# Parameters made in two parts by channel, the first for the first two chunks of the generation

## The chip, the cores and the metric

One core of one Trainium2 chip. The core has TensorE (PE), VectorE (DVE), ScalarE (ACT), GpSimd (POOL) and SyncE (SP), which issues DMAs; GpSimd and ScalarE issue DMAs too. Each engine works through its own instructions in order and waits on semaphores for the others. The metric is the device time of one execution in microseconds; shorter is better.

## The reference

Two branches over one sequence of 2,048 tokens and 640 channels are mixed by a gate. Branch A is attention of 32 heads over a window of 8 positions, two apart. Branch B is a state space layer: a long kernel K per channel, made from 192 complex states, then convolved with the input by FFT.

```python
def _A_ref(x, wqkv, wo):
    qkv = (x @ wqkv)                       # q, k, v: H = 32, Dh = 20
    logits = einsum("bhsd,bhswd->bhsw", q, kg) * Dh ** -0.5   # W = 8, dil = 2
    attn = softmax(where(mask, logits, -1e9))
    return einsum("bhsw,bhswd->bhsd", attn, vg) @ wo

def _B_ref(u, A_re, A_im, B_re, B_im, C_re, C_im, log_dt, Dskip):
    dt = exp(log_dt)
    P = exp(dt * (A_re + 1j * A_im) * l)   # 640 x 192 states x 2048
    K = einsum("dn,dnl,dn->dl", C, P, dt * B).real
    y = irfft(rfft(u padded) * rfft(K padded))[:L] + u * Dskip
...
g = sigmoid((x * gate_w).sum(-1, keepdims=True))
return g * _A_ref(x, ...) + (1 - g) * _B_ref(x, ...)
```

## The kernel before

The program has three stretches. In the first, `SSMParams.build` turns the six parameter arrays into 12 bfloat16 "pieces" per state: phase, phase times 256, log decay, log size and angle, each split into two or three parts (`split`, `piece`). It works on all 640 channels at once, as tiles of 128 partitions by 5 x 192 columns (the 960-wide instructions). Each piece is copied on ScalarE (L352) and written to the DRAM buffer `Sprm` by SP (L353). Between its 22 steps stand the steps of `Attn.window`: transposes of x on TensorE (L86) with copies to `xT` on ScalarE (L87), the projections to q, k and v of the first 1,024 tokens (L117, copies of two at a time at L119, written to DRAM by GpSimd at L122), and the gate (L93 to L105).

In the second stretch, `KGen.chunk` generates the long kernel in 10 chunks of 64 channels. `load_L` reads a chunk's pieces back from `Sprm` into one of two tiles L, by 8 DMAs on SP (L449). TensorE multiplies them with constants to give arguments in PSUM (L471, two `ar` buffers), ScalarE takes 12 sines (L482, `trg`) and 6 exponentials (L488, `exq`) of them per chunk, VectorE multiplies the two (L504 to L506, into `pt` and `qq`), and TensorE contracts over the states into `kps` (L515). Even chunks take the sines first, odd chunks the exponentials, so that ScalarE's table is loaded once per change of function. After five chunks `KExpand.expand` spreads the values to 2,048 positions by way of DRAM.

Each of the 18 sines and exponentials of a chunk ends in `drain`, which advances a tick (180 ticks in all) and calls `tick_hook`. The hook puts other work between: projections of the last 1,024 tokens (`proj_late`, L148 to L152, 30 of them, 0.42 per tick) and steps of the attention (`Attn.core`, 88 steps, 0.47 per tick after the first six). The core's steps are the scores (products on VectorE at L189, sums on TensorE at L191, softmax at L197 to L206), the mix (L221, L224, L225) and the output projection (L234, L235). `proj_late`, the mix and the output projection use the same PSUM tile name, `tb`, in a pool with one buffer; the scores use `lg`, also one. The scheduler of the tile framework decides the final order on each engine by priority and by what is ready, so an instruction can stand somewhat off the tick that emitted it.

The third stretch, `fft_conv`, transforms input and kernel (L615, L703), multiplies the spectra on VectorE (L716 to L721), transforms back (L732, copies to C at L655 and L657; L745) and adds the gated attention (L750 to L756). Half of the kernel's first transform is done ahead, between chunks (`f1_half`, L842, L843). The weights wqkv and `xT` lie in `bufA`, which later holds the kernel's transform `Bk` and then C.

What sets the order around the change: the DMA queues of SP (parameter loads, x, pieces, L reads, in this order of issue) and of GpSimd (wqkv, constants, projections out, attention in); the tick rates; the single buffers of `tb` and `lg`; and `bufA`.

Of the kernel before, what the change touches and what calls it, by code (L numbers as in the profile page):

```python
# [21 lines left out]
D = 640  # L22
H = 32
DH = 20
W = 8
# [22 lines left out]
class Attn:  # L48
# [22 lines left out]
    def window(self, wk, cst, pa, g_sb):  # L71

        nc = self.nc
        xn, xT, wq, ident = self.xn, self.xT, self.wq, self.ident
        steps = []

        def zeros():
            zz = cst.tile([128, 5, HALO], BF16, name="zz")
            nc.vector.memset(zz[:], 0.0)
            nc.gpsimd.dma_start(self.kS[:, :, 0:HALO], zz[:])  # L80
            nc.gpsimd.dma_start(self.vS[:, :, 0:HALO], zz[:])

        def transpose(hf, kt):
            tx = pa.tile([128, 2, 512], F32, name="ar")
            for i in range(8):
                nc.tensor.matmul(tx[:, i // 4, (i % 4) * 128:(i % 4) * 128 + 128], xn[:, 8 * hf + i, kt * 128:(kt + 1) * 128], ident[:], start=True, stop=True)  # L86
            nc.scalar.activation(xT[:, kt, 1024 * hf:1024 * hf + 1024], tx[:].rearrange("p a b -> p (a b)"), ACT.Identity)  # L87

        def gate():
            gz = pa.tile([128, 2, 512], F32, name="ar")  # L90
            for i in range(16):
                for kt in range(NKT):
                    nc.tensor.matmul(gz[:, 0, i:i + 1], xT[:, kt, i * 128:(i + 1) * 128], self.gw[:, kt:kt + 1], start=(kt == 0), stop=(kt == NKT - 1))  # L93
            ge = cst.tile([128, 16], F32, name="ge")
            nc.scalar.activation(ge[:], gz[:, 0, 0:16], ACT.Exp, scale=-1.0)
            nc.vector.tensor_scalar(ge[:], ge[:], 1.0, None, ALU.add)
            nc.vector.reciprocal(g_sb[:], ge[:])
            omg = cst.tile([128, 16], F32, name="omg")
            nc.vector.tensor_scalar(omg[:], g_sb[:], -1.0, 1.0, ALU.mult, ALU.add)
            ob = cst.tile([128, 16], BF16, name="ob")  # L100
            nc.vector.tensor_copy(ob[:], omg[:])
            nc.tensor.matmul(gz[0:16, 1, 0:128], ob[:], ident[:], start=True, stop=True)
            om2 = cst.tile([16, 128, 2], BF16, name="om2")
            nc.scalar.activation(om2[:], gz[0:16, 1, 0:128].unsqueeze(2).to_broadcast([16, 128, 2]), ACT.Identity)
            nc.gpsimd.dma_start(self.omS.rearrange("(i p) t -> i (p t)", p=128), om2[:].rearrange("i p t -> i (p t)"))  # L105
        cur = {}

        def proj(sc, j):
            if j == 0:
                cur["t"] = wk.tile([128, 15, SC], BF16, name="prjw")  # L110
            t = cur["t"]
            n = min(2, 15 - j)
            pp = pa.tile([128, 2, 512], F32, name="ar")
            for k in range(n):
                which, e = divmod(j + k, 5)
                for kt in range(NKT):
                    nc.tensor.matmul(pp[:, k], wq[:, kt, which * D + e:(which + 1) * D:5], xT[:, kt, sc * SC:sc * SC + SC],  # L117
                                     start=(kt == 0), stop=(kt == NKT - 1))
            nc.scalar.activation(t[:, j:j + n, :], pp[:, 0:n], ACT.Identity)  # L119
            for which, (dstS, off) in enumerate(((self.qS, 0), (self.kS, HALO), (self.vS, HALO))):  # L120
                if j <= 5 * which + 4 < j + n:
                    nc.gpsimd.dma_start(dstS[:, :, off + sc * SC:off + sc * SC + SC], t[:, 5 * which:5 * which + 5])  # L122
        steps.append(zeros)
        for kt in range(NKT):
            steps.append(lambda kt=kt: transpose(0, kt))
        for j in range(0, 15, 2):
            steps.append(lambda j=j: proj(0, j))
        for kt in range(NKT):
            steps.append(lambda kt=kt: transpose(1, kt))
        for j in range(0, 15, 2):  # L130
            steps.append(lambda j=j: proj(1, j))
        steps.append(gate)
        return steps

    def proj_late(self, wk, ps):

        nc = self.nc
        for sc in range(2, NSC):
            c0 = sc * SC
            for which, dstS, off in ((0, self.qS, 0), (1, self.kS, HALO), (2, self.vS, HALO)):  # L140
                for e in range(5):
                    if e % 2 == 0:
                        n = min(2, 5 - e)
                        t = wk.tile([128, 2, SC], BF16, name="prj", tag="PHI", bufs=3)
                    pp = ps.tile([128, 2, 256], F32, name="tb")
                    ppf = pp[:].rearrange("p a b -> p (a b)")
                    for kt in range(NKT):
                        nc.tensor.matmul(ppf, self.wq[:, kt, which * D + e:(which + 1) * D:5], self.xT[:, kt, c0:c0 + SC],  # L148
                                         start=(kt == 0), stop=(kt == NKT - 1))
                    nc.scalar.activation(t[:, e % 2, :], ppf, ACT.Identity)  # L150
                    if e % 2 == n - 1:
                        nc.gpsimd.dma_start(dstS[:, e + 1 - n:e + 1, off + c0:off + c0 + SC], t[:, 0:n])  # L152
                    yield
# [112 lines left out]

def _arg_consts():
# [36 lines left out]
class SSMParams:  # L304

    def __init__(self, ctx, tc):
        dr = ctx.enter_context(tc.tile_pool(name="sp_dram", bufs=1, space=DRAM))
        self.S = dr.tile([D, NPC, NST], BF16, name="Sprm")

    def build(self, ctx, tc, A_re, A_im, B_re, B_im, C_re, C_im, log_dt, gate_w, ident, gw_sb, pa, xl, wl):  # L310
        nc = tc.nc
        pin = ctx.enter_context(tc.tile_pool(name="sp_in", bufs=1, side="right"))
        pcs = ctx.enter_context(tc.tile_pool(name="sp_pc", bufs=4, side="right"))
        SH = [128, 5, NST]
        t = {}

        def load(eng, nm, ap):
            t[nm] = pin.tile(SH, BF16, name=nm)
            eng.dma_start(t[nm][:], ap.rearrange("(k p) n -> p k n", p=128))
        lg10 = pin.tile([10, 128], BF16, name="lg10")  # L320
        nc.sync.dma_start(lg10[0:5], log_dt.rearrange("(k p) -> k p", p=128))
        nc.sync.dma_start(lg10[5:10], gate_w.rearrange("(k p) -> k p", p=128))
        load(nc.sync, "cre", C_re); load(nc.scalar, "bre", B_re)
        load(nc.sync, "cim", C_im); load(nc.scalar, "bim", B_im)
        xl[0]()
        load(nc.sync, "aim", A_im)
        xl[1]()
        for w_ in wl:
            w_()
        load(nc.sync, "are", A_re)  # L330
        xl[2](); xl[3]()
        f = lambda nm: pin.tile(SH, F32, name=nm)
        dtb = pin.tile([128, 5], BF16, name="dtb")
        dt2 = pin.tile([128, 5], F32, name="dt2")
        dtB = dtb[:].unsqueeze(2).to_broadcast(SH)
        lt = pa.tile([128, 2, 512], F32, name="ar")
        nc.tensor.matmul(lt[:, 0, 0:10], lg10[:], ident[0:10, 0:10], start=True, stop=True)
        nc.scalar.activation(dtb[:], lt[:, 0, 0:5], ACT.Exp)
        nc.scalar.activation(gw_sb[:], lt[:, 0, 5:10], ACT.Identity)
        V, SCA = nc.vector, nc.scalar  # L340
        Sv = self.S.rearrange("(k p) i n -> p k i n", p=128)
        t0, t1, wr, wi, ax, ay = (f(n) for n in ("t0", "t1", "wr", "wi", "ax", "ay"))
        tau, x1, xa, xl_, at, s0, s1 = (f(n) for n in ("tau", "x1", "xa", "xl", "at", "s0", "s1"))
# [6 lines left out]
        def piece(cur, nxt, i):  # L350
            pc = pcs.tile(SH, BF16, name="pc")
            SCA.activation(pc[:], cur[:], ACT.Identity)  # L352
            nc.sync.dma_start(Sv[:, :, i, :], pc[:])  # L353
            if nxt is not None:
                V.tensor_tensor(nxt[:], cur[:], pc[:], ALU.subtract)
# [5 lines left out]
        W = []  # L361
        def weights():
            TT(wr[:], t["cre"][:], t["bre"][:], ALU.mult)
            TT(t0[:], t["cim"][:], t["bim"][:], ALU.mult)
            TT(wi[:], t["cre"][:], t["bim"][:], ALU.mult)
            TT(t1[:], t["cim"][:], t["bre"][:], ALU.mult)
# [4 lines left out]
            TT(dt2[:], dtb[:], dtb[:], ALU.mult)  # L371

        def phase():
            TT(tau[:], t["aim"][:], dtB, ALU.mult)
            wrap(tau, tau, U16, s0)

        def ratio():
# [5 lines left out]
            SCA.activation(at[:], t1[:], ACT.Arctan)  # L383
# [5 lines left out]
        def size():  # L389
            TT(xl_[:], xl_[:], xa[:], ALU.add)  # L390
            TT(xl_[:], xl_[:], dt2[:].unsqueeze(2).to_broadcast(SH), ALU.mult)
            V.tensor_scalar(xl_[:], xl_[:], 1e-36, None, ALU.max)
            SCA.activation(xl_[:], xl_[:], ACT.Ln)

        def angle1():
            TT(t0[:], ay[:], ax[:], ALU.is_gt)
            V.tensor_scalar(t1[:], at[:], -2.0, float(np.pi / 2), ALU.mult, ALU.add)
            TT(t1[:], t1[:], t0[:], ALU.mult)
            TT(at[:], at[:], t1[:], ALU.add)

        def angle2():
            V.tensor_scalar(t0[:], wr[:], 0.0, None, ALU.is_lt)
# [524 lines left out]
```

## Time and profile before

| | us |
|---|---|
| median of three runs | 451.12 (449.47 to 454.13) |
| profiled execution, its own time | 452.35 |
| its span | 450.6 |
| first piece issued to `Sprm` / last one | 22.55 / 61.2 |
| first read of L issued / first argument matmul | 65.6 / 71.0 |
| last sine of chunk 9 | 335.1 |
| last copy of `kps` to E over | 341.4 |
| TensorE / ScalarE / VectorE busy | 351.3 / 326.2 / 315.4 |

The span is cut into 40 slices, and a digit is the busy share of a slice in tenths; PEclk is the clock that TensorE was granted, in tenths of full speed. A group's line gives the source line, the engine, the output and input tiles and their shapes. In a timeline, the first number is the start, the second the duration of the merged instructions, and the square bracket tells how long the engine was idle before and what released it. Matmuls overlap in the pipeline, so a busy TensorE is not one at its peak.

### The profile page before, as it was taken

To read this page: it belongs to the slowest core of one execution; us is meant where nothing else is said; L and a number is where in the kernel's file an instruction comes from. 1 tells how busy PE (TensorE), PEld (TensorE's weight loads), DVE (VectorE), ACT (ScalarE), POOL (GpSimd) and SP (SyncE) were. 2 spreads that over 40 slices of the span, in tenths; PEclk is the share of its full clock that TensorE was granted. 3 is DMA by queue.
4 is the path that set the end of the run, shared out by engine and by line. 5 is a ranking of instruction groups with operands and counts; after the bars stand their busy time and mean duration, and the time that the engine had idled before them with its cause. 6 is when DMAs were issued, how large, how long until landed. Compare 5 with 4: busy or idle time off the path is not lost.

```text
span 450.6 us, 11334 instructions
## 1 busy us (share of the span) xinstructions
PE 351.3 (78%) x4886; PEld 199.3 (44%) x4886; DVE 315.4 (70%) x378; ACT 326.2 (72%) x456; POOL 80.3 (18%) x113
## 2 busy tenths in 40 slices
PE   0497798664898989997998778988976579995981
PEld 0343454222354354443444234544545565553971
DVE  5698910489896597474799686767365756998783
ACT  1668968656468887659698398999873559895783
POOL 8811012621112301220510000000000000000034
PEclk9998998865799999996999596988995989999798
DMA  8935555734334552733946412311017492214137
GB/s 285 359 82 175 152 168 131 240 88 120 108 87 124 165 114 80 187 96 77 267 161 205 160 35 66 94 25 49 31 56 280 148 197 78 71 35 125 65 70 165
DMA packets 59413, 58.80 MB, mean 130 GB/s; under 512 B 44628, under 2 KB 51300, under 8 KB 59108
## 3 DMA queue, kind: packets, MB, share of 16 engines
q1 hardware_dynamic: 49828, 29.51, 24.8%
q0 software_dynamic: 7920, 26.74, 19.8%
q10 hardware_dynamic: 1616, 1.84, 1.2%
q8 instruction: 38, 0.62, 0.6%
q14 instruction: 11, 0.09, 0.1%
HBM read 38.29 MB, written 19.77 MB: 129 GB/s over the span
## 4 chain that ended last, share of the span: by engine, by line
PE 28%; ACT 21%; DVE 12%; DMA 3%; issue 3%; POOL 0%; ACTq 0%; SPq 0%; POOLq 0%; DVEq 0%
PE tb L224 5%; PE tb L148 5%; PE fp L703 4%; ACT trg L482 4%; PE ar L471 4%; PE tb L234 3%; DVE bufA L657 3%; ACT sp_u L706 2%; ACT sp_k L706 2%; ACT exq L488 2%; ACT ga L235 2%; PE bp L615 2%; DMA kc<-Kx 2%; ACT L482 2%; DVE prod L189 2%
## 5 line engine op out<-in xcount | busy, mean ns | idle before, releaser
L482 ACT ACTIVATE trg<-ar 128x608 bf16<-128x608 int16 x120 | 76.2, 680 | 12.6 <-PE ar L471 11.9
L471 PE MATMUL ar<-Rarg,L 64*128 64x304 bf16 (+1 forms) x480 | 65.7, 302 | 15.6 <-ACT exq L488 7.6
L189 DVE TENSOR_TENSOR prod<-qc,kc 128x2048 bf16<-128x2048 bf16 x40 | 47.6, 1210 | 24.4 <-DMA qc<-qS 12.5
L221 DVE TENSOR_TENSOR pv<-vc,asb 128x4096 bf16<-128x4096 bf16 (+1 forms) x24 | 46.1, 1931 | 19.2 <-PE tb L224 17.8
L488 ACT ACTIVATE exq<-ar 128x864 bf16<-128x864 f32 x60 | 50.6, 898 | 9.9 <-DVE qq L506 7.6
L224 PE MATMUL tb<-pv,ident 128*128 128x512 bf16 (+1 forms) x192 | 44.0, 368 | 4.6 <-DVE pv L221 2.7
L148 PE MATMUL tb<-bufA 128*128 128x512 bf16 x150 | 41.5, 399 | 4.9 <-ACT ga L235 2.5
L471 PEld LDWEIGHTS <-L 64*128 64x128 bf16 x480 | 24.2, 96 | 46.7 <-issue 41.7
L515 PE MATMUL kps<-qq,pt 128*32 128x22 bf16 (+1 forms) x2560 | 37.9, 177 | 8.7 <-DVE qq L506 6.4
L515 PEld LDWEIGHTS <-pt 128*32 128x32 bf16 (+1 forms) x2560 | 26.5, 93 | 35.6 <-issue 27.2
L117 PE MATMUL ar<-bufA 128*128 128x512 bf16 x150 | 35.9, 403 | 5.0 <-ACT prjw L119 3.2
L504 DVE TENSOR_TENSOR pt<-trg,exq 128x1024 bf16<-128x1024 bf16 x30 | 20.5, 684 | 25.2 <-ACT trg L482 19.0
L703 PEld LDWEIGHTS <-PHI 128*128 128x128 bf16 x256 | 24.8, 97 | 18.5 <-issue 8.3
L234 PE MATMUL tb<-wo_sb,oT 128*128 128x320 bf16 x160 | 30.0, 323 | 2.0 <-ACT ga L235 1.0
L191 PE MATMUL lg<-prod,ind 128*32 128x512 bf16 x160 | 23.5, 448 | 8.0 <-DVE prod L189 5.0
L150 ACT ACTIVATE prj<-tb 128x512 bf16<-128x512 f32 x30 | 17.9, 596 | 15.3 <-PE tb L148 13.3
L224 PEld LDWEIGHTS <-ident 128*128 128x128 bf16 x192 | 18.7, 102 | 21.6 <-issue 9.2
L117 PEld LDWEIGHTS <-bufA 128*128 128x128 bf16 x150 | 18.1, 121 | 22.6 <-issue 8.0
L506 DVE TENSOR_TENSOR qq<-trg,exq 128x1408 bf16<-128x1408 bf16 x30 | 26.5, 883 | 0.0
L634 POOL DMA_DIRECT2D PHI<-c_phi x8 | 4.4, 549 | 118.7 <-PE fp L703 118.7
L148 PEld LDWEIGHTS <-bufA 128*128 128x128 bf16 x150 | 16.7, 119 | 18.5 <-issue 8.7
L225 ACT ACTIVATE oT<-tb 128x512 bf16<-128x512 f32 (+1 forms) x24 | 12.6, 525 | 14.7 <-PE tb L224 14.7
(191 smaller groups left out, 621.4 us busy)
## 6 DMA issues: line engine op xcount, KB each, us to landing
asb<-aS SPq DMA_DIRECT2D x8, 512.0 KB, 3.9
PSI<-c_psi SPq DMA_DIRECT2D x8, 512.0 KB
PHI<-c_phi POOLq DMA_DIRECT2D x8, 384.0 KB, 3.6
Sprm<-pc SPq DMA_DIRECT2D x12, 240.0 KB, 2.3
L<-Sprm SPq DMA_DIRECT2D x80, 36.0 KB, 3.2
kc<-kS POOLq DMA_DIRECT2D x8, 337.5 KB, 5.1
vc<-vS POOLq DMA_DIRECT2D x8, 337.5 KB, 5.2
xn<-in_A_x_dram SPq DMA_DIRECT2D x4, 640.0 KB, 12.1
```

What stands on the lines that cost most here:

```text
L117: nc.tensor.matmul(pp[:, k], wq[:, kt, which * D + e:(which + 1) * D:5], xT[:, kt, sc * SC:sc * SC + SC], start=(kt == 0), stop=(kt == NKT ...
L148: nc.tensor.matmul(ppf, self.wq[:, kt, which * D + e:(which + 1) * D:5], self.xT[:, kt, c0:c0 + SC], start=(kt == 0), stop=(kt == NKT - 1))
L189: nc.vector.tensor_tensor(prod[:], qc[:, e, :].unsqueeze(1).to_broadcast([128, W, C]), win(kc[:, e, :], 0, W, DIL, C), ALU.mult)
L221: nc.vector.tensor_tensor(pv[:, :, 0:n, :], for_e, asb[:].unsqueeze(2).to_broadcast([128, W, n, C]), ALU.mult)
L224: nc.tensor.matmul(op[:, 0:n, :], ident[:], pv[:, w, 0:n, :], start=(w == 0), stop=(w == W - 1))
L234: nc.tensor.matmul(apf[:, :320], oT[:, e, i * 128:(i + 1) * 128], wo_sb[:, e, hf * 320:(hf + 1) * 320], start=(e == 0), stop=(e == 4))
L471: nc.tensor.matmul(ar[:, g2, a0:a0 + ncol], L[rows, gp, sub, m0:m0 + 128], R[rows, c0:c0 + ncol], start=True, stop=True, tile_position=(64 ...
L482: nc.scalar.activation(dst[:, 2 * gp:2 * gp + 2, sub, :], ar[:].bitcast(I16)[:, :, 0:2 * SW:2], ACT.Sin, scale=SCL)
L488: nc.scalar.activation(dst[:, 2 * gp:2 * gp + 2].rearrange("p g s n -> p g (s n)"), ar[:, :, 0:2 * EW], ACT.Exp)
L506: V.tensor_tensor(qq[:], trg[:, :, KI:].rearrange("p a (v m) -> p a v m", v=2), exq[:, :, KI:].unsqueeze(2).to_broadcast([128, 32, 2, NM]) ...
L515: nc.tensor.matmul(kps[32 * g:32 * g + 32, c2, NM * ql:NM * ql + NM], pt[rows, 8 * g + ql, v, :], qq[rows, 8 * g + ql, v, :], start=(key n ...
L703: nc.tensor.matmul(fp[:, fl, 0:320].rearrange("p (c x) -> p c x", x=32), PHI[:, fl, kind, :], B[:, :, 2 * f1 + ri].rearrange("p c q g -> p ...
```

## The change

The 640 channels are assigned anew to chunks, through `chan(c, q)`, so that channel 5p + k lies on partition p: the parameter loads read whole rows, and slice k of the tiles holds the channels of chunks 2k and 2k + 1. `build` becomes `loads` and `part`. Part A (k = 0) is made at once on tiles of 192 columns, its 12 pieces go out in five DMAs, and L is read for chunks 0 and 1. Part B (k = 1 to 4, tiles of 768 columns) gives seven steps before the generation and one per tick from then on; its Arctan and Ln are held until the first chunk's six exponentials are issued (`between`), and the sines after that are ordered behind them (`after`). The even chunks now take the exponentials first. The comparisons that pick the angle's quadrant become signs on ScalarE.

The window keeps only the transposes of the first 1,024 tokens. All 60 projections (15 per 512 tokens) and the other transposes move into the ticks: one per tick up to tick 30, then 0.4 per tick; until tick 25 they take turns between the PSUM tiles `lg` and `tb`. Each of them is copied alone (512 columns). The gate is made at tick 31. The attention's core is created when part B is through, and its steps run from tick 26 on, 0.56 per tick. `f1_half` moves from chunks 5 to 9 to chunks 7 and 8, five each. In the FFT, C is written with four columns five elements apart in place of four adjacent ones. The constants and memsets of `KGen` are issued ahead of the loads on GpSimd.

```diff
-    def proj_late(self, wk, ps):
+    def slot(self):
+        self.nslot += 1
+        if self.turns and self.nslot % 2:
+            t = self.ps.tile([128, W, 64], F32, name="lg")
+        else:
+            t = self.ps.tile([128, 2, 256], F32, name="tb")
+        return t[:].rearrange("p a b -> p (a b)")
...
+    def late(self, wk):
+        yield from self.proj(wk, 0)
         for sc in range(2, NSC):
...
+            yield from self.transposes(sc)
+        for sc in range(1, NSC):
+            yield from self.proj(wk, sc)
...
+def chan(c, q):
+    return 40 * (c % 2) + 5 * q + c // 2
...
-            eng.dma_start(t[nm][:], ap.rearrange("(k p) n -> p k n", p=128))
...
+            eng.dma_start(t[nm][:], ap.rearrange("(p k) n -> p k n", k=5))
...
+    def part(self, pool, tc, k0, nk, hold):
+        SH = [128, nk, NST]
...
+            SCA.activation(pc, cur[:], ACT.Identity)
+            if pc1 is None:
+                nc.sync.dma_start(Sv[:, :, i, :], pc)
+            elif i in last:
+                nc.sync.dma_start(Sv[:, 0, last[i]:i + 1, :], pc1[:, last[i]:i + 1, :])
...
+            hold(lambda: SCA.activation(at[:], t1[:], ACT.Arctan))
...
+        def signs():
+            TT(t0[:], ax[:], ay[:], ALU.subtract)
+            SCA.activation(ax[:], t0[:], ACT.Sign)
+            SCA.activation(wr[:], wr[:], ACT.Sign)
+            SCA.activation(wi[:], wi[:], ACT.Sign, bias=eps[:])
...
-        first, second = (0, 1) if c % 2 == 0 else (1, 0)
+        first, second = (1, 0) if c % 2 == 0 else (0, 1)
         for u in range(3):
             gen(u, first)
+        prev = self.last
+        for f in self.between:
+            ins = f()
+            after(self.tc, ins, prev)
+            prev = ins
+        self.since = prev if self.between else None
...
-            dst = C.rearrange("p x (c q) -> p x c q", c=2)[:, :, :, 4 * cb:4 * cb + 4]
+            x0 = chan(cb // 2, 4 * (cb % 2))
+            dst = C.rearrange("p x (c q) -> p x c q", c=2)[:, :, :, x0:x0 + 16:5]
...
+    with tc.tile_pool(name="sp_A", bufs=1, side="right") as pA:
+        for st_ in prm.part(pA, tc, 0, 1, lambda f: f()):
+            st_()
+    Ls = {0: kg.load_L(0), 1: kg.load_L(1)}
+    psteps = prm.part(pB, tc, 1, 4, kg.between.append)
+    at.window(acst, pa)
+    for st_ in range(7):
+        psteps.pop(0)()
...
         def tick_hook():
             state["n"] += 1
-            late_to(int(state["n"] * 0.42))
-            while state["k"] < 6 + int(state["n"] * 0.47) and not state["done"]:
+            n = state["n"]
+            if psteps:
+                psteps.pop(0)()
+                if not psteps:
+                    c1.close()
+                    at.load_wo()
+                    state["core"] = at.core(c2, g_sb, ps, lambda sc: late_to((15, 40, 55, 70)[sc]))
+            late_to(n if n < 30 else 30 + int((n - 30) * 0.4))
+            if n == 31:
+                at.gate(acst, g_sb)
+            if n == 25:
+                at.turns = False
+            if state["core"] and n > 25:
+                while state["k"] < 2 + int((n - 25) * 0.56) and not state["done"]:
...
-            if c >= HC:
-                k0 = 3 * (c - HC)
-                extra += [lambda n=n: f1_half(n) for n in range(k0, min(k0 + 3, 2 * HC))]
+            if c in (7, 8):
+                extra += [lambda n=n: f1_half(n) for n in range(HC * (c - 7), HC * (c - 6))]
```

## The prediction

> **What bounds the kernel now.** I read the page first, then the stretches by stage, then the chain of waits in order of time, then the tile that the chain keeps returning to. The page's slices are 11.27 us each (450.6 / 40):
>
> ```profile
> PE   0497798664898989997998778988976579995981
> DVE  5698910489896597474799686767365756998783
> ACT  1668968656468887659698398999873559895783
> PEclk9998998865799999996999596988995989999798
> ```
>
> No engine is full for long. To price the change I need stages. ScalarE runs one sine (L482) or exponential (L488) per tick, 18 per chunk, so counting them in its timeline dates every tick: tick 1 ends near 73, tick 18 (chunk 0 done) at 95.7, tick 30 at 115.1, tick 72 at 183.0, tick 180 at 335.1, and the last copy to E is over at 341.4. The columns below are PE, PEld, DVE, ACT, POOL busy us, granted clock, DMA share, GB/s:
>
> ```profile
> 0.00:71.00 71.00, 46.82 (x316) 26.97 (x316) 47.05 (x46) 46.62 (x50) 26.26 (x37) 0.98 0.65 200
> 71.00:115.10 44.10, 29.16 (x383) 11.20 (x381) 28.04 (x36) 29.28 (x43) 13.26 (x18) 0.69 0.50 140
> 115.10:183.00 67.90, 62.36 (x948) 31.26 (x948) 51.11 (x60) 49.95 (x80) 14.09 (x18) 0.98 0.45 122
> 183.00:235.00 52.00, 46.52 (x689) 22.61 (x683) 35.60 (x37) 39.50 (x61) 12.98 (x17) 0.93 0.55 148
> 235.00:341.40 106.40, 86.85 (x1735) 45.96 (x1735) 71.90 (x95) 85.28 (x126) 1.72 (x2) 0.87 0.30 93
> 341.40:450.60 109.20, 79.56 (x828) 61.27 (x827) 81.72 (x108) 75.53 (x99) 11.99 (x21) 0.91 0.47 114
> ```
>
> Stage 1 (0 to 71) is parameters, transposes, 30 projections; each engine idles a third of it. Then come ticks 1 to 30 at a clock of 0.69, the dense part, and the FFT (109.2 us, nearly untouched). The chain says what ends last in the middle:
>
> ```profile
> PE 28%; ACT 21%; DVE 12%; DMA 3%; issue 3%; POOL 0%; ACTq 0%; SPq 0%; POOLq 0%; DVEq 0%
> PE tb L224 5%; PE tb L148 5%; PE fp L703 4%; ACT trg L482 4%; PE ar L471 4%; PE tb L234 3%; DVE bufA L657 3%; ACT sp_u L706 2%; ACT sp_k L706 2%; ACT exq L488 2%; ACT ga L235 2%; PE bp L615 2%; DMA kc<-Kx 2%; ACT L482 2%; DVE prod L189 2%
> ```
>
> L148, L224 and L234 share one PSUM tile, tb, with a single buffer. The timeline shows a ping-pong, five matmuls, then the copy, then the next five, 1.92 to 1.97 us from start to start:
>
> ```profile
> 144.46 1.24 PE L148 MATMUL tb<-bufA 128*128 128x512 bf16 x5 [0.32 <-ACT prj L150]
> 145.73 0.60 ACT L150 ACTIVATE prj<-tb 128x512 bf16<-128x512 f32 x1 [0.76 <-PE tb L148]
> 146.38 1.24 PE L148 MATMUL tb<-bufA 128*128 128x512 bf16 x5 [0.17 <-ACT prj L150]
> 147.71 0.60 ACT L150 ACTIVATE prj<-tb 128x512 bf16<-128x512 f32 x1 [0.24 <-ACT trg L482]
> 148.35 1.24 PE L148 MATMUL tb<-bufA 128*128 128x512 bf16 x5
> ```
>
> How full that one slot is, is the sum of PE and ACT busy on tb, since they alternate: 83%, 81% and 64% of these stretches.
>
> ```profile
> 138.08:199.20 61.12, 35.44 (x158) 15.44 (x27) 1.00 0.50 126
> 131.60:216.00 84.40, 46.91 (x207) 21.52 (x38) 0.96 0.50 125
> 95.70:183.00 87.30, 38.87 (x173) 17.10 (x31) 0.87 0.43 114
> ```
>
> So while projections and attention run together, the tb slot paces the kernel; later, with attention alone, ScalarE does (85.28 of 106.4 us in all, and chunks 7 to 9 take 21.8 us each, with some 20 us of ScalarE work in each).
>
> **The change part by part.** *Start of the generation.* Before, the first argument matmul is at 71.0. After, it needs the five pieces-DMAs of part A and eight L reads. Part A's VectorE work: 37 instructions on 192 instead of 960 columns, about 0.3 us each from the 960-wide rows (1.15 and 0.65) cut to a fifth plus some 0.07 fixed, one of them a reciprocal of 1.3 (6.14 / 5): 12 us. In the changed program's order, 13 of part B's instructions (768 wide, 0.55 to 0.9 us, some 10 us) stand among them, and the Arctan of part A stands behind the first transpose copy on ScalarE, so behind xn. Its queues: cre still lands about 5; aim, read at 15.4 before behind an xn load, comes earlier; wqkv moves on POOL's queue behind 8.3 us of memsets, which leaves bandwidth to xn and costs nothing while projections wait for transposes (up to 8 us if they did not). 5 + 12 + 10 and some 3 us of waits gives 30 for the last piece. From the last piece to the first argument matmul it was 9.8 us before (61.2 to 71.0). So 39; bounds 34 and 45. While that matmul waits, 12 of the first 15 projections stand behind it on TensorE, and their copies are in the next sum.
>
> *Ticks 1 to 18* hold 15 projections less the three ahead of the first arguments, three transposes, and part B on ScalarE. Its sum there, from the order: 6 exponentials x 0.82, 12 sines x 0.60, 11 projection copies x 0.5, 3 transpose copies x 0.5, 13 parameter instructions x 0.72 (960-wide rows start 0.90 apart, times 0.8), 4 table loads x 1.28: 33.7 us. TensorE has about 20, VectorE 27 (part B's reciprocal 4.9). ScalarE is the bound; at 95% it is 35. Sign has no row; between nothing and a table load each it is 0 to 8 us, and I take Square's and Abs's 0.99 scaled, since the order shows no extra table load. Two new waits: part B's Arctan and Ln stand behind the sixth exponential and the sines behind them, and its reciprocal is ready near 36, ahead of the first exponential, so 0; part B's pieces stand on SP's queue behind 16 L reads of 0.43 us, 7 us, and with three pc buffers ScalarE's fourth piece may wait 0 to 3 us, inside the 95%. *Ticks 19 to 30*: 12 x 0.6 + 12 copies x 0.5 + a table, 14.5, I take 16. Tick 30 is then at 39 + 35 + 16 = 90, against 115.1.
>
> *What was put off.* At tick 30, before has 18 projections and 68 of 88 attention steps to do; after has 40 and 84, and the gate (2.1 us of matmuls at 68.9). This gives most of the 25 us back. Ticks 31 to 130 use tb for 40 projections x 1.84 (1.24 + 0.60) = 73.6, and 56 attention steps = 5.1 rounds of (2 x 2.50 + 1.41 + 4 x 1.37 = 11.9) = 60.6: 134 us. At 82% full, the two dense rows' value, 164 us; at 64%, 210; at 95%, 141. I take 82% because the mix of work is that of 131 to 216, and there is more of it per tick, not less. Add 2 for the gate and 3 for the first half's expansion, whose 5 us of VectorE copies now fall into this dense part.
>
> *Ticks 131 to 180*: 2.78 chunks x 21.8 = 60.6, plus 6.5 more attention steps x 0.5 of ScalarE = 3.3, plus 3 more f1 copies x 0.93 (their place moves to chunks 7 and 8, since bufA now holds the weights longer): 67. Then 6 to the last copy, as before. Sum 90 + 164 + 2 + 3 + 67 + 6 = 332 against 341.4: 9.4 us less.
>
> *FFT.* The columns of C are now written five elements apart, 20 copies. A nearest row:
>
> ```profile
> 421.93 9.14 DVE L657 CAST bufA<-cp 128x1024 bf16<-128x1024 f32 x8 [0.48 <-PE cp L732]
> ```
>
> These read PSUM 512 bytes apart at 1.14 us for 1,024 elements and are not slowed by it; I take 0. Doubled, the ten on VectorE cost 11 us on the path. Here a rule speaks against the change: the Trainium skill, "SBUF — State Buffer", section "Door 1: The DMA port swizzle", has 16-byte lines and a penalty for each access that enters a new one. By it, four elements 10 bytes apart touch three lines where before they touched one, so the estimate would lean to the 11 us; the row shows a stride that is free, but on PSUM and for reading.
>
> Small edits with one answer: fewer Dskip DMAs, sign arithmetic in place of comparisons (7 fewer VectorE instructions), contiguous parameter loads, 30 more projection copies split in two: under 1 us on the path, hidden by the ScalarE and tb bounds above.
>
> **The rivals.** (1) *Slower: the tb slot becomes the dam.* 45 of 60 projections go through tb one at a time, where before 30 ran 2 per copy through two ar buffers at about 2.15 us a pair. For it: 64% filling at 95 to 183, where VectorE's queue stood in the way. Against it: that stretch had a half clock, 81 to 83% followed. At 70% ticks 31 to 130 take 191, the E copy is at 359, the time 17.6 later: 469. It decides below 79% filling against my start. (2) *The gain is given back exactly*: filling 78 to 79% or the start at 45 plus expansion 5: 450. (3) *The spaced writes cost 11*: 442 + 11 = 453. (4) *Larger gain*: filling 90% (149) and no cold stretch later: 332 - 15 - 3, time 424. For it: the clock is 0.69 in ticks 1 to 30 and 0.87 after 235, and denser TensorE work would keep it up. (5) *Part B is not hidden*: chunk 2 needs its pieces at tick 37, they end near tick 20, so it takes a ScalarE sum twice 33.7 before this counts; I give it little.
>
> **How the numbers follow.** The profiled execution took 452.35 with a span of 450.6; the median of three is 451.1, so 9.4 less gives a span of 441.2, a profiled time of 443, and 442 by the median. Chances: forecast 0.40 (433 to 447), larger gain 0.17, given back 0.15, tb dam 0.18, spaced writes 0.06, part B or a late start 0.04. A measurement here tells about 1% from no change (446.6 to 455.6). Faster: 0.17 + 0.38 of the forecast's 0.40 = 0.55; within: 0.15, the forecast's other 0.02 and 0.02 of the spaced writes = 0.19; slower: 0.18 + 0.04 + 0.04 = 0.26. Likeliest case alone: 433 to 447. For eight in ten I keep the larger gain to 426 and the dam to 464.
>
> **What would show it.** Right: first L498 at 34 to 45; 18th sine or exponential 35 us later with ScalarE over 90% busy; tick 30 near 90; PE plus ACT on tb at 80% or more over ticks 31 to 130; clock near 1.0 there; last E copy near 332; L693 casts still 1.14. Wrong: ScalarE waiting on L142's tb while tb fills under 75%, VectorE behind L188 holding trg buffers as at 95 to 110 before, or casts of 2 us.

## The result and the profile after

The changed kernel takes 471.86 us (median of four runs, 468.3 to 476.38), the kernel before beside it 452.0 (449.47 to 454.13): a ratio of 1.0415, interval 1.0316 to 1.0515. The ratio is worked out without the longest of the four, a slow run. The kernel is slower, and the time lies outside the predicted range. The profiled execution took 468.3 us with a span of 466.5. The generation gained 5 us; the FFT lost four times as much.

The slices of the kernel after (11.66 us each), and its chain:

```profile
PE   1557499988986989996899988778685799666480
DVE  5996746778688454869846697832585598989972
PEclk9979599889997999999999999997988999955586
...
PE 35%; ACT 26%; DVE 18%; issue 9%; DMA 8%; POOL 2%; ACTq 0%; SPq 0%; POOLq 0%; DVEq 0%
PE tb L140 10%; DVE bufA L693 8%; PE tb L223 5%; PE fp L739 4%; PE ar L498 3%; ACT exq L516 3%; ACT prj L142 3%; PE tb L233 3%; ACT trg L509 3%; ACT sp_u L742 2%; ACT sp_k L742 2%; PE lg L190 2%; PE lg L140 2%; PE bp L651 2%; DMA kc<-kS 2%
```

Two things stand out. In slices 36 to 38 (408 to 443 us) VectorE is at 8 and 9 tenths, TensorE at 6, 6 and 4, and the granted clock is at 0.5. And VectorE's copy into bufA, 3% of the chain before, has 8%.

The same execution by stage, in the columns of the prediction's windows (PE, PEld, which is TensorE's loading of weights, DVE, ACT, POOL busy, granted clock, DMA share, GB/s); the borders are the first sine or exponential, tick 30, tick 130, tick 180, the last E copy, and the two ends of the copies to C:

```profile
0.00:37.00 37.00, 15.84 (x72) 7.73 (x73) 30.94 (x60) 24.83 (x45) 20.64 (x31) 0.91 0.76 250
37.00:83.50 46.50, 36.86 (x448) 17.33 (x447) 28.64 (x38) 43.96 (x70) 11.49 (x16) 0.85 0.50 144
83.50:250.80 167.30, 145.36 (x2233) 73.21 (x2232) 118.06 (x146) 120.31 (x189) 36.68 (x49) 0.96 0.50 138
250.80:330.30 79.50, 67.27 (x1090) 35.72 (x1090) 53.43 (x57) 64.23 (x96) 4.67 (x7) 0.96 0.23 66
330.30:337.00 6.70, 2.95 (x222) 2.55 (x222) 2.88 (x7) 1.05 (x2) 0.00 (x0) 1.00 0.15 51
337.00:410.00 73.00, 56.91 (x384) 40.39 (x383) 57.51 (x75) 53.78 (x49) 2.71 (x5) 0.95 0.58 143
410.00:444.50 34.50, 18.94 (x317) 16.86 (x318) 32.43 (x11) 31.71 (x10) 0.00 (x0) 0.50 0.08 31
444.50:466.50 22.00, 10.56 (x128) 10.21 (x128) 11.18 (x22) 11.59 (x40) 9.26 (x16) 0.73 0.55 120
```

The row 410 to 444.5 is the one to read: both copying engines are busy over nine tenths of it, TensorE 55%, at half its clock. The timeline of that stretch:

```profile
410.82 4.61 PE L768 MATMUL cp<-GAB,Y 64*128 64x128 bf16 x76 [2.06 <-DVE Y L757]
411.95 31.71 ACT L691 ACTIVATE bufA<-cp 128x1024 bf16<-128x1024 f32 x10 [5.36 <-PE cp L768]
412.74 31.67 DVE L693 CAST bufA<-cp 128x1024 bf16<-128x1024 f32 x10 [1.98 <-PE cp L768]
416.37 1.89 PE L768 MATMUL cp<-GAB,Y 64*128 64x128 bf16 x32 [0.93 <-DVE bufA L693]
419.74 1.90 PE L768 MATMUL cp<-GAB,Y 64*128 64x128 bf16 x32 [1.48 <-DVE bufA L693]
...
444.47 6.46 PE L782 MATMUL yp<-bufA,PSI 128*128 128x160 bf16 x72 [3.42 <-DVE bufA L693]
```

The ten copies of each engine stand end to end, 31.7 us in all; TensorE does two groups of 16 matmuls in 1.9 us and then waits 1.48 for a buffer of cp. Before, a copy took about a third as long, and TensorE ran through:

```profile
416.59 12.89 PE L732 MATMUL cp<-GAB,Y 64*128 64x128 bf16 x316 [2.06 <-DVE Y L721]
431.12 5.16 PE L745 MATMUL yp<-bufA,PSI 128*128 128x160 bf16 x72 [1.64 <-DVE bufA L657]
```

Where the time went, by the same events in both profiles (each dated by its start; the last E copy before starts at 341.40 and is over at 341.93):

| stretch, us | before | after | difference |
|---|---|---|---|
| start to last E copy | 341.4 | 336.4 | -5.0 |
| last E copy to the long row of cp matmuls | 75.2 | 74.4 | -0.8 |
| that row to the first yp matmul | 14.5 | 33.65 | +19.1 |
| first yp matmul to the end | 19.5 | 22.0 | +2.5 |
| span | 450.6 | 466.5 | +15.9 |

### The profile page after: what moved, and what is told of

It is laid out like the page before. It is cut to its first block, busy times and chain, and to the rows that moved or that the text cites. A ratio compares the mean times of both kernels' runs of the same rounds, so it can differ in the third digit from the quotient of the medians.

```text
span 466.5 us, 11435 instructions
## 1 busy us (share of the span) xinstructions
PE 354.7 (76%) x4886; PEld 204.0 (44%) x4886; DVE 335.1 (72%) x409; ACT 351.5 (75%) x498; POOL 85.4 (18%) x123
## 4 chain that ended last, share of the span: by engine, by line
PE 35%; ACT 26%; DVE 18%; issue 9%; DMA 8%; POOL 2%; ACTq 0%; SPq 0%; POOLq 0%; DVEq 0%
PE tb L140 10%; DVE bufA L693 8%; PE tb L223 5%; PE fp L739 4%; PE ar L498 3%; ACT exq L516 3%; ACT prj L142 3%; PE tb L233 3%; ACT trg L509 3%; ACT sp_u L742 2%; ACT sp_k L742 2%; PE lg L190 2%; PE lg L140 2%; PE bp L651 2%; DMA kc<-kS 2%
## 5 line engine op out<-in xcount | busy, mean ns | idle before, releaser
L509 ACT ACTIVATE trg<-ar 128x608 bf16<-128x608 int16 x120 | 79.5, 695 | 3.6 <-PE ar L498 3.4
L498 PE MATMUL ar<-Rarg,L 64*128 64x216 bf16 (+1 forms) x480 | 63.7, 291 | 18.7 <-ACT trg L509 11.4
L140 PE MATMUL tb<-bufA 128*128 128x512 bf16 x260 | 72.3, 405 | 5.8 <-ACT prj L142 4.1
L142 ACT ACTIVATE prj<-tb 128x512 bf16<-128x512 f32 x52 | 31.3, 601 | 26.8 <-PE tb L140 16.2
L550 PE MATMUL kps<-qq,pt 128*32 128x22 bf16 (+1 forms) x2560 | 41.5, 177 | 4.5 <-DVE qq L541 3.1
L223 PE MATMUL tb<-pv,ident 128*128 128x512 bf16 (+1 forms) x192 | 41.3, 352 | 4.0 <-DVE pv L220 2.3
L691 ACT ACTIVATE bufA<-cp 128x1024 bf16<-128x1024 f32 x10 | 31.7, 3514 | 5.4 <-PE cp L768 5.4
L693 DVE CAST bufA<-cp 128x1024 bf16<-128x1024 f32 x10 | 31.7, 3414 | 2.0 <-PE cp L768 2.0
L768 PE MATMUL cp<-GAB,Y 64*128 64x128 bf16 x320 | 19.3, 307 | 16.5 <-DVE bufA L693 11.3
L768 PEld LDWEIGHTS <-Y 64*128 64x128 bf16 x320 | 17.0, 141 | 18.8 <-issue 13.1
```

Source lines behind the costliest of these rows:

```text
L223: nc.tensor.matmul(op[:, 0:n, :], ident[:], pv[:, w, 0:n, :], start=(w == 0), stop=(w == W - 1))
L498: nc.tensor.matmul(ar[:, g2, a0:a0 + ncol], L[rows, gp, sub, m0:m0 + 128], R[rows, c0:c0 + ncol], start=True, stop=True, tile_position=(64 ...
L509: ins = nc.scalar.activation(dst[:, 2 * gp:2 * gp + 2, sub, :], ar[:].bitcast(I16)[:, :, 0:2 * SW:2], ACT.Sin, scale=SCL)
L550: nc.tensor.matmul(kps[32 * g:32 * g + 32, c2, NM * ql:NM * ql + NM], pt[rows, 8 * g + ql, v, :], qq[rows, 8 * g + ql, v, :], start=(key n ...
L693: nc.vector.tensor_copy(o, i)
```

## The experiments

**The writes alone, undone and done.** Two theories: the spaced columns of C cost the 19 us; or the order and the load of the FFT had changed in some other way. The first kernel is the one after with the columns of C adjacent again. The channels stay where the change puts them; only the column of Y that each matmul reads is chosen so that four neighbours of C come out together.

```diff
+def ycol(d):
+    return 16 * (d % 5) + 8 * (d // 40) + d % 40 // 5
...
-  Y[64 * c2:64 * c2 + 64, ro, 4 * cb + l, :],
+  Y[64 * c2:64 * c2 + 64, ro, ycol(4 * cb + l), :],
...
-            x0 = chan(cb // 2, 4 * (cb % 2))
-            dst = C.rearrange("p x (c q) -> p x c q", c=2)[:, :, :, x0:x0 + 16:5]
+            dst = C.rearrange("p x (c q) -> p x c q", c=2)[:, :, :, 4 * cb:4 * cb + 4]
```

> The changed kernel with one thing undone: each copy into C takes four columns that are adjacent in C again; the matmuls before it pick the matching columns of Y, so the result is the same. Theory 1 (the spaced writes alone make it slower): the 20 copies fall from 3.4 to 1.14 us (VectorE) and 1.02 (ScalarE), the stretch from first cp matmul to first yp matmul from 33.7 to 14.5 us, the clock at its end recovers and gives 2 more, and the time is 472 - 21 = 450, ratio to before 0.985 to 0.995. Theory 2 (the generation and its tail make it slower, the slow copies only stand where there was slack): the time stays above 465.

451.15 us, a ratio of 0.993 (0.9884 to 0.9976) to before. Its two groups of copies, and the matmuls ahead of them and behind them:

```profile
L698 DVE CAST bufA<-cp 128x1024 bf16<-128x1024 f32 x10 | 11.5, 1218 | 2.5 <-PE cp L773 2.5
L696 ACT ACTIVATE bufA<-cp 128x1024 bf16<-128x1024 f32 x10 | 10.1, 1023 | 6.8 <-PE cp L773 6.3
```

```profile
414.94 12.32 PE L773 MATMUL cp<-GAB,Y 64*128 64x128 bf16 x316 [1.85 <-DVE Y L762]
428.90 5.15 PE L786 MATMUL yp<-bufA,PSI 128*128 128x160 bf16 x72 [1.64 <-DVE bufA L698]
```

From the first of the long row of cp matmuls (414.94) to yp it is 13.96 us. The whole loss of that row is gone with the spacing.

The second kernel is the one before, with nothing but the spaced writes added:

```diff
+            x0 = 20 * (cb // 5) + cb % 5
-  Y[64 * c2:64 * c2 + 64, ro, 4 * cb + l, :],
+  Y[64 * c2:64 * c2 + 64, ro, x0 + 5 * l, :],
-  dst = C.rearrange("p x (c q) -> p x c q", c=2)[:, :, :, 4 * cb:4 * cb + 4]
+  dst = C.rearrange("p x (c q) -> p x c q", c=2)[:, :, :, x0:x0 + 16:5]
```

> The kernel before with the spaced writes alone: groups of four columns of C that lie five elements apart, Y's columns picked to match, the same result. Theory 1: copies of 3.4 us, cp to yp 33.7 in place of 14.5, time 452 + 19 to 22 = 471 to 474, ratio 1.04 to 1.05. Theory 2: under 456.

475.57 us, 1.0512 (1.0453 to 1.0571). Spacing alone makes the kernel before as slow as the one after; the row of cp matmuls starts at 417.84 and yp at 451.67, 33.83 us later:

```profile
L655 ACT ACTIVATE bufA<-cp 128x1024 bf16<-128x1024 f32 x10 | 31.9, 3505 | 5.4 <-PE cp L733 5.4
L657 DVE CAST bufA<-cp 128x1024 bf16<-128x1024 f32 x10 | 31.8, 3439 | 2.0 <-PE cp L733 2.0
```

**What the price depends on.** Either each 16-byte line of SBUF that a group of four columns enters is paid for, or every element that is not next to the last one costs the same, or the two engines hinder each other when both write spaced. So the same edit to the kernel before with other distances, two, four and twenty columns (x0 = 4·st·(cb // st) + cb % st, a step of st), and with five once more, but all twenty copies on VectorE:

```diff
-  copy_on(nc, cb, dst, cp[:].rearrange("p c l x -> p x c l"))
+  copy_on(nc, 1, dst, cp[:].rearrange("p c l x -> p x c l"))
```

> The same with columns two elements (4 bytes) apart, so the four lie within 16 bytes. Theory A (the cost goes with 16-byte lines entered): copies stay at 1.0 to 1.2 us, time as before. Theory B (every element that is not adjacent to the last costs the same): 3.4 us as at five, time about 471.

> The kernel before with the four columns of C four elements (8 bytes) apart. Theory A, a price per 16-byte line entered: two apart enters a new line at a quarter of the elements and took 1.1 cycles of 0.96 GHz per element (1.14 us), five apart at seven tenths and took 3.15 (3.36 us), so some 4.5 cycles per line entered; four apart enters one at half of them: 2.25 cycles, 2.4 us per VectorE copy, time about 465. Theory B, a price for any element outside the 8 bytes of the one before: 3.4 us as at five.

> The same with 20 elements (40 bytes) apart, a new 16-byte line at every element. Theory A: 4.5 cycles, 4.8 us per copy, time about 487. Theory B: 3.4 us, about 474.

> Five apart as above, with all 20 copies on VectorE, one after the other. If each copy's own writes cost 3.4 us, they still do, and the stretch from cp to yp takes 68 us, the time 505 or so. If the two engines hinder each other, VectorE alone takes 1.1 to 2 us per copy, and the stretch 24 to 40.

The line of VectorE's copies in each (shortest/median/longest ns, then first and last start). Two apart:

```profile
L657 DVE CAST bufA<-cp x10: 1227/1250/1281, 423.7 to 434.5; 128x1024 bf16<-128x1024 f32 x10
```

Four apart:

```profile
L657 DVE CAST bufA<-cp x10: 2368/2406/2408, 418.8 to 438.6; 128x1024 bf16<-128x1024 f32 x10
```

Five apart, in the kernel after:

```profile
L693 DVE CAST bufA<-cp x10: 2401/3660/3670, 412.7 to 442.0; 128x1024 bf16<-128x1024 f32 x10
```

Twenty apart:

```profile
L657 DVE CAST bufA<-cp x10: 4812/5088/5234, 415.1 to 456.0; 128x1024 bf16<-128x1024 f32 x10
```

Five apart, all on VectorE:

```profile
L657 DVE CAST bufA<-cp x20: 2369/3623/3637, 417.5 to 477.7; 128x1024 bf16<-128x1024 f32 x20
```

| columns apart | 16-byte lines that four columns enter | VectorE, median us | per line of the 256 groups, ns | time, us |
|---|---|---|---|---|
| 1 | 1 | 1.22 | (at most 4.8) | 452 |
| 2 | 1 | 1.25 | (at most 4.9) | 456.74, one run |
| 4 | 2 | 2.41 | 4.7 | 463.62, one run |
| 5 | 3 (2 where the first starts a line) | 3.66 (2.40) | 4.8 (4.7) | 471.86 (kernel after; 475.57 before with these writes) |
| 20 | 4 | 5.09 | 5.0 | 483.68, one run |

A copy writes 1,024 elements in 256 groups of four; from two lines per group on, the time is 256 x lines x 4.7 to 5.0 ns. At one line per group something else is the limit: the copies into Bu write 16 adjacent elements at a time, enter 128 lines in all, and take the same 1.22 us. The two durations inside "five apart" follow the same rule: a group that begins at the start of a line takes bytes 0, 10, 20 and 30 and enters two lines, any other enters three. Two apart is 4 bytes apart and stays within one line, and its copies are free on VectorE, so spacing as such is not what costs. (That run's 456.74 does not come from them: from cp to yp it takes 14.0 us, but its last E copy comes 6.4 us later than before.) ScalarE has much the same steps: means of 1.02 us adjacent, 1.29 two apart, 2.47, 3.51 and 5.16. On VectorE alone a copy takes what it takes beside ScalarE (3.62 against 3.66), so it isn't that the two hinder each other; that kernel takes 502.55, since twenty such copies now stand in one row.

**What sets the pace of the generation.** With adjacent writes the new order gives 0.7% (0.2 to 1.2) and no more: its generation ends 2.2 us earlier than before (last E copy at 339.16 against 341.40), where the prediction had 9.4. The prediction had let the tb slot pace ticks 31 to 130 and ScalarE's sum pace ticks 131 to 180. Three kernels, all built on the one with adjacent writes, take one suspect each. (The kernel with adjacent writes and the kernel after have the same generation and differ by 2.2 us at tick 180; less than 3 us between two profiles isn't read.)

First, more attention early, so that less of it is left for the last ticks:

```diff
-  while state["k"] < 2 + int((n - 25) * 0.56) and not state["done"]:
+  while state["k"] < 2 + int((n - 25) * 0.64) and not state["done"]:
```

> The changed kernel with adjacent writes and the attention's steps at 0.64 per tick in place of 0.56, so that they are emitted by tick 160 or so and not at tick 180. Theory G1 (ticks 131 to 180 take 80 us and not 67 because the attention's last rounds, each a chain through DRAM, are left to the last two chunks): ticks 131 to 180 at 72 or less, ticks 31 to 130 longer by at most 5, time 3 to 6 less than with 0.56 (ratio to before 0.98 to 0.987). Theory G2 (the sum of the work on ScalarE and TensorE sets it): what is gained after tick 130 is lost before, ratio 0.99 to 1.0.

452.72 us, 1.0064 (1.0023 to 1.0105). Ticks 31 to 130 take 173.3 (169.7), ticks 131 to 180 take 81.8 (79.8): nothing came back at the end. But the edit took little attention out of the last ticks. The matmuls and copies on tb in ticks 131 to 180, with adjacent writes alone and with 0.64:

```profile
252.70:332.50 79.80, 34.73 (x167) 15.07 (x28) 0.96 0.24 67
257.30:339.20 81.90, 31.38 (x151) 13.50 (x25) 0.86 0.31 98
```

The 40 matmuls of the scores (tile lg) stand there in both, and the granted clock is lower, 0.86 in place of 0.96. So this run does not settle whether the attention left over lengthens the last ticks.

Second, the first half's ten `f1_half` copies taken out of chunks 7 and 8 and done in the FFT, where the second half's are:

```diff
-                    if hf == 0:
-                        half["kc"] = kx.load(0, kk)
...
-            if c in (7, 8):
-                extra += [lambda n=n: f1_half(n) for n in range(HC * (c - 7), HC * (c - 6))]
...
+            K0 = kx.load(0, kcp0)[:].rearrange("p a b -> p (a b)")
+            for c in range(HC):
+                fft_f1(nc, ps1, lambda ql: K0[:, 8 * c + ql::HC * CQ], F1c, Bk, c, 0)
```

> The changed kernel with adjacent writes, and the ten first transforms of the first kernel half moved out of chunks 7 and 8 into the FFT stretch, behind those of the input, where TensorE waits some 7 us for the kernel's second half from DRAM. Theory G3 (those ten copies of 1 us on ScalarE, in a stretch that ScalarE and their single PSUM buffer pace, cost 13 us in ticks 131 to 180): those ticks at 68 to 72, the FFT stretch 0 to 4 longer, time 5 to 10 less, ratio 0.97 to 0.983. Theory G1: chunk 9 stays at 34 or more, ratio 0.988 to 1.0.

456.7 us, 1.0179 (1.0093 to 1.0265), where 0.97 to 1.0 was expected. The last ticks do shrink, from 79.8 to 65.4:

```profile
256.20:321.60 65.40, 53.84 (x945) 27.51 (x943) 46.93 (x51) 52.51 (x81) 4.67 (x7) 0.95 0.27 76
```

Not all of that is the ten copies: these ticks also hold less attention, 31 matmuls on lg in place of 40 and 147 on tb in place of 167. Ticks 31 to 130 took 172.2 here, so tick 180 comes 10.9 earlier, and the FFT gives that back: 86.2 us from the last E copy to the row of cp matmuls, in place of 75.8. A longer wait for a read of the convolution's kernel (Kx) is 4 us of it; the first line is with adjacent writes alone, the second is this kernel:

```profile
358.82 6.55 PE L656 MATMUL bp<-F1c,kc 128*128 128x256 bf16 x36 [4.26 <-DMA kc<-Kx]
352.02 2.76 PE L656 MATMUL bp<-F1c,kc 128*128 128x256 bf16 x12 [8.28 <-DMA kc<-Kx]
```

So the same with that first half read early, into a tile of its own, by GpSimd's queue:

```diff
+        kc0 = kcp0.tile([128, 64, CH], BF16, name="kc0")
+        for g in range(4):
+            nc.gpsimd.dma_start(kc0[32 * g:32 * g + 32].rearrange("p t c -> p (t c)"),
+                                kx.Kx[0, :, g].rearrange("h (a b) x -> h a (b x)", a=4))
```

> As the run that moved the ten first transforms of the kernel's first half into the FFT stretch, but that half is read back from DRAM on GpSimd's queue into its own place, ahead of the end of the generation and not behind the second half on SP's queue. Theory G3 (the ten copies cost some 11 us in ticks 131 to 180, and can lie under the wait for the second half): last sine or exponential near 322, the transforms between 344 and 352, the second half's transforms from 350 on, time 5 to 9 less than with them in the generation, ratio to before 0.975 to 0.985. If the wait does not cover them: ratio 0.99 to 1.02, as when they stood behind the second half.

455.88 us, 1.0123 (1.006 to 1.0186): not the 0.975 to 0.985 hoped for, but the other case of the expectation, in which the wait does not cover the copies. Ticks 131 to 180 are short again (65.8), ticks 31 to 130 longer (178.7), and the stretch ahead of cp takes 83.9. Waits at the second half's read stay, one of ScalarE, which issues part of it ahead of its next copy, and one of TensorE:

```profile
353.69 1.02 ACT L696 ACTIVATE Bu<-bp 128x1024 bf16<-128x1024 f32 x1 [5.36 <-DMA kc<-Kx]
...
363.04 1.59 PE L656 MATMUL bp<-F1c,kc 128*128 128x256 bf16 x12 [3.31 <-DMA kc<-Kx]
```

Reading the first half early did not remove them. Why ticks 31 to 130 grew by 9 us here isn't settled (the 2.5 of the run before it are too few to read).

Third, tb relieved: from tick 25 on every projection and transpose goes through the two `ar` buffers that the sines' arguments use.

```diff
-        if self.turns and self.nslot % 2:
+        if not self.turns:
+            return self.pa.tile([128, 2, 512], F32, name="ar")[:, 0]
+        if self.nslot % 2:
```

> The changed kernel with adjacent writes, and the 40 projections after tick 25 taking one of the two PSUM tiles ar (which the generation's arguments use) in place of the single tile tb. Theory T (the one tb slot paces ticks 31 to 130, 170 us there at 80% full): tb's demand falls from 134 to 60 us, those ticks take 150 to 158, the time falls by 8 or more, ratio to before 0.975 or less. Theory W (the sum of TensorE's and ScalarE's work paces them, and tb is full because it stands on the same path): those ticks stay within 5 us of 170, ratio 0.985 to 1.005.

446.41 us, 0.9878 (0.983 to 0.9926). Matmuls and copies on tb over ticks 31 to 130, with adjacent writes only:

```profile
83.00:252.70 169.70, 89.49 (x437) 39.33 (x70) 0.94 0.49 136
```

and with the projections on ar:

```profile
86.30:252.70 166.40, 45.20 (x222) 17.48 (x34) 0.95 0.49 136
```

Half the work has left the slot, which is now 38% full in place of 76%, and these ticks are 3.3 us shorter of 169.7. A slot that paces would have let go of far more; the expectation had 150 to 158 us. The test has one flaw: the work went to ar, whose two buffers are busier for it (180 us of matmuls and copies in these ticks in place of 108), and TensorE's waits for ScalarE to free a buffer of ar rise from 7.2 to 11.1 us. So some of the gain may have been given back there, but these 4 us are not the 12 and more that were expected. Tick 30 came 3.3 later, ticks 131 to 180 took 75.4 in place of 79.8, and the last E copy is at 334.95, 4.2 earlier. This kernel and the one with adjacent writes lie below both kernels of the change, though below the kernel before by less than 2%. This one has the lowest median of all, but the intervals of the two ratios to before overlap (from 0.9884 to 0.9926).

## Why the prediction was wrong

| step, us | predicted | after | off by |
|---|---|---|---|
| to the first argument matmul | 39 | 33.0 | -6.0 |
| from there to tick 18 | 35 | 36.2 | +1.2 |
| ticks 19 to 30 | 16 | 14.3 | -1.7 |
| ticks 31 to 130, gate and expansion with them | 169 | 167.3 | -1.7 |
| ticks 131 to 180 | 67 | 79.5 | +12.5 |
| to the last E copy | 6 | 6.1 | +0.1 |
| FFT | 109.2 | 130.1 | +20.9 |
| span | 441.2 | 466.5 | +25.3 |

**The step that failed is the FFT's: "These read PSUM 512 bytes apart at 1.14 us for 1,024 elements and are not slowed by it; I take 0."** The row showed a stride where data is read, from PSUM; the change puts one where it is written, to SBUF. The row bore on another operand and was no bound for this one. The copies went from 1.22 to 3.66 us, ten of them on each engine, and the pace of the stretch passed from TensorE (two groups in 1.3 us) to the copies (two groups in 3.38): 19.1 us. The kernel before with this one edit pays it all, and the kernel after without it pays none: there the FFT, from the last E copy to the end, takes 110.6 us, and 109.2 were forecast. Its time, 451.15, is still above the likeliest range of 433 to 447, by what the last ticks take (below).

**The rule that spoke against it was right.** The Trainium skill, "SBUF — State Buffer", section "Door 1: The DMA port swizzle", has 16-byte lines, with a penalty for an access that enters a new one. The prediction quoted it, counted three lines in place of one, and weighed it below the row. From one line to four the durations go up by one step for every line, as the rule says. In one point the runs differ from the same passage: it holds that two hits in a line are enough for full bandwidth, and gives eight bf16 as the distance that can be strided for free; four apart has two hits in each line and costs 2.41 us in place of 1.22. The measurement decides: of the distances tried, only two apart, four hits in a line, was free (on VectorE; ScalarE's copies went from 1.02 to 1.29 us).

**The third rival had the mechanism, not the size.** It doubled the copies and came to 11 us. Counted by lines, the same rule would have tripled most of them: VectorE's ten copies took 31.7 us in place of 11.6, 20.1 more, of which 19.1 came on the path; before, TensorE set the pace and VectorE waited 2.9 us for it. The tail behind is 2.5 us longer than before, and 1.3 of that are its yp matmuls. They start at half clock after the spaced row and take 10.9 us; before they take 9.6, and the same with adjacent writes:

```profile
444.47:455.35 10.88, 10.59 (x128) 10.24 (x128) 8.44 (x16) 8.95 (x32) 4.94 (x9) 0.87 0.49 101
431.12:440.75 9.63, 9.29 (x128) 8.95 (x128) 8.31 (x16) 8.86 (x32) 4.91 (x9) 1.00 0.55 113
```

**The start** was 6 us better than forecast, and at 33.0 just outside its bounds of 34 and 45. Most of that is one term, the wait from the last piece to the first argument, which was taken over from before at 9.8 us. Here it is 4.4: the last piece is issued at 28.6 (30 was forecast), the first read of L 1.8 later (4.4 before), and the first matmul starts 2.6 after that (5.4 before). **Ticks 1 to 30** were right: 50.5 us for 51, and ScalarE, which the sum took as the bound, was busy for 43.96 of the 46.5 us from the first exponential on.

**Ticks 31 to 130** came out right for a wrong reason. tb's work was 127.6 us, not 134, and the slot was 76% full, not 82%; the errors cancel:

```profile
83.50:250.80 167.30, 88.25 (x461) 39.34 (x70) 0.96 0.50 138
```

With the slot at 38% the time hardly moves. TensorE is the fullest engine there (145.36 of 167.3 us), but that it sets the pace was not tested. The reading "one buffer, alternating, 82% full, so it paces" was the error.

**Ticks 131 to 180** are the second term that was off, by 12.5 us. The prediction made ScalarE's work the time of this stretch. It took 6.5 more attention steps at 0.5 us of ScalarE each, 3.3 us, and put their work on TensorE and VectorE at nothing. The same ticks before:

```profile
273.70:335.60 61.90, 53.44 (x1022) 29.20 (x1016) 36.52 (x45) 56.18 (x85) 0.86 (x1) 0.90 0.18 51
```

After (the row 250.80:330.30 above) the stretch is 17.6 us longer, with 8 us more work on ScalarE, 13.8 more on TensorE and 16.9 more on VectorE. On the tiles tb and lg (the attention, and after also three late projections) TensorE works 41.8 us in place of 27.1. ScalarE is also idle for 9.6 us more, and waits most for the attention's matmuls:

```profile
ACT oT L224 <- PE tb L223: 6.9, 5, 3.4
ACT ga L234 <- PE tb L233: 4.3, 6, 0.9
```

(The columns are total, number of times and longest, in us, of ScalarE's waits in ticks 131 to 180 after; before, the same two were 1.6 and 0.9.) So the term for the attention was too small; that its work is what lengthened the stretch is likely and not shown, since no run took it out of these ticks alone. The other term, "3 more f1 copies x 0.93", is a small part at most: taking all ten copies out, and some attention with them, shortened the stretch by 14.4, at most 1.4 each, so for three at most 4.3 in place of 2.8, or 1.5 of the 12.5.

## What to carry to other kernels

When an edit changes the pattern of a write, count the 16-byte lines that its groups enter and take the price from a row that writes that way; a stride on the read side prices nothing on the write side. When data must land in a new order, look for the index that is free to permute ahead of the write: here the column of Y that a matmul takes as its weights, which cost nothing (cp to yp 13.96 us, against 14.5 before). And a single buffer that is three quarters full and stands on the chain is a suspect, not yet the pace; it is tested by giving half its work another buffer.

## What the runs showed of the hardware

- In these bf16 copies from PSUM, VectorE and ScalarE pay 4.7 to 5.0 ns for every 16-byte line that a group enters, once it enters two or more. Up to four elements in a line come at the price of one: on VectorE 1.22 us for 1,024 adjacent elements, 1.25 two apart, 2.41 four apart, 5.09 twenty apart. ScalarE, faster when adjacent (1.02), has no advantage any more four apart (2.47).
- How long the granted clock stayed at 0.50 went with TensorE's waits. In both kernels of the change it was at 0.50 when the row of cp matmuls began, behind some 6 us with little work on TensorE (0.43 of 5.6 us before, 0.65 of 5.8 after). Without waits in the row it was back near 1.00 after 5.4 us; with waits of 1.48 us in every 3.38 it stayed at 0.50 for the whole row, 410 to 444.5 us. With waits of 0.80 and 0.15 in every 2.21 us (columns four apart) it came back to 1.00 too. The rows are those of the kernel before, at the start of its cp matmuls and from then on, and of the one with columns four apart:

```profile
416.60:422.00 5.40, 5.40 (x102) 5.40 (x104) 2.52 (x3) 2.98 (x3) 0.00 (x0) 0.50 0.35 142
422.00:431.10 9.10, 7.25 (x218) 6.32 (x215) 9.07 (x8) 7.05 (x8) 0.00 (x0) 0.99 0.02 4
```

```profile
422.60:437.30 14.70, 8.78 (x224) 6.71 (x223) 14.70 (x8) 14.70 (x7) 0.00 (x0) 1.00 0.01 2
```

In the spaced row the copies set the pace, so the half clock cost nothing there; the yp matmuls behind it, begun at half clock, took 10.9 us in place of 9.6.
